# One attention-and-FFN kernel on one core: the plan's transfers re-costed, and the order of all engines drawn anew

## The chip, the core and the metric

The kernel runs on one core of a Trainium2 chip. The core has a matrix engine (PE, with its weight loads shown apart as PEld), a vector engine (DVE), a scalar engine (ACT), GpSimd (POOL), and a sync engine (SP) that here does nothing but issue transfers. The metric is the device time of one execution, in microseconds (us). Three executions of the kernel before took 928.43, 929.65 and 935.46 us.

## The reference, cut to what matters

```python
# q, k, v: 8 batches x 8 heads x 576 x 64;  omega: 128 x 64
def phi(x):
    h = x @ omega.T - sum(x * x) / 2
    return exp(h - max(h)) / sqrt(128)
kv  = phi(k).T @ v                      # per head, 128 x 64
z   = phi(k).sum(over the sequence)
out = (phi(q) @ kv) / (phi(q) @ z + 1e-6)
x   = out as 4608 tokens x 512
y   = gelu_erf(x @ w_in) @ w_out        # 512 -> 2048 -> 512
```

## The kernel before, in words

The attention is cut into 32 units of two heads (`u0` to `u31`, four a batch). The FFN is cut into 18 blocks of 256 tokens; block n can start when the batches that hold its tokens are through attention. Units `u0` to `u7` are worked in fp32 (`pair`, `shared`, `kv`, `q_trans`, `num_plain`); from `u8` on, and from block 1 on, each fp32 factor is split into a high and a low half and multiplied in three passes (`proj`, `kv_split`, `num`, `product`, `mm2`). Blocks use a seven-product scheme for the first FFN product (`sw1`, then `comb_a` on ACT and `comb_b`, `comb_c` on DVE, then `sw2`). The weights come in 16 pieces of 1 MB (`w_load`), each rebuilt on ACT, DVE and POOL (`w_hi`, `w_lo`, `w_shift`, `w_round`, `w_max`) before use, and split later (`w_low` and others).

Nothing is scheduled at run time. The kernel first lists all operations with `op(engine, cost, function, ...)`, and each takes a number from the table `RANK` (L36). `Planner.run` (L275) sorts the operations of each engine by that number, and each engine works in that order on the chip: an instruction whose inputs are late holds all that stands behind it on its engine. The costs serve three ends only: the sequence in which engines' operations are written down, which of several PSUM rings a result goes to, and the fillers. A filler is a matmul of no use, written by `put` (L1515) ahead of a PE operation for which the plan sees over 0.9 us of idle time:

```python
if X['fill'] and o.idle > 0.9 and o.t > 5.0:
    for _ in range(int((o.idle - 0.3) * X['fill'] / 0.11) if t else 0):
        nc.tensor.matmul(t[0][:, 0:256], id16[:, 0:P], id16, start=True, stop=True)
```

Transfers go out on SP's queue, in SP's order; only the transposed keys of `u0` and `u1`, and half of omega, go out on ACT's queue (`load_two` L746, `load_om` L517). SP and ACT each issue in their own order. DVE and POOL share a port to SBUF for some operations, which the planner knows by the names in `PORT` (L211) and by `port` in `run`.

Of the kernel before, what the change touches and what calls it, by code (L numbers as in the profile page):

```python
# [19 lines left out]
P = 128  # L20
# [10 lines left out]
X = dict(pm=0.15, tsw=1.28, psw=0.057, pst=0.3, plain=8, tiles=6, fill=0.6, kvp=8, eb0=8, amax=0, tc=1.2, tx=2.0)  # L31
# [4 lines left out]
RANK = (1, 0, 0, 0, 0, 1, 2, 2, 4, 6, 1, 4, 2, 3, 1, 3, 6, 6, 6, 8, 10, 12, 9, 7, 14, 21, 24, 3, 10, 15, 12, 16, 11, 14, 14, 20, 17, 23, 0, 3, 7, 2,  # L36
# [192 lines left out]
class Planner:  # L229
# [10 lines left out]
    def op(self, e, c, fn, *a, r=(), w=(), new=(), due=None, kind=None, tab=None, size=0, after=None, deps=()):  # L240
        o = Op()
# [136 lines left out]
def favor_attention_ffn(ctx: ExitStack, tc: tile.TileContext, qT, kT, v, omT, w_in, w_out, out):  # L378
# [12 lines left out]
    R2 = 2 * S  # L391
# [519 lines left out]
    def unit_plain(u):  # L911
        for s in range(2):
            op('SP', 0.05 if u.k < 2 and s == 0 else 0.45, load_two, u, s, w=[('x', s, u.k % 2)], size=295e3)
# [640 lines left out]
```

## Time and profile before

| | before |
|---|---|
| median of three runs | 929.65 us |
| lowest, highest | 928.43, 935.46 us |
| the profiled execution | 928.76 us |
| its span in the trace | 927.0 us |
| PE busy | 906.2 us, 98% of the span |
| ACT, DVE, POOL busy | 741.4, 736.2, 554.4 us |

A busy PE is one that has a matmul in its pipeline; matmuls overlap. The idle time that the views give before a group is that of its engine, with the work that ended it behind the arrow. The span is 1.8 us shorter than the execution's time.

### The profile page before, as it was taken

What the parts mean: (1) busy time and instruction counts of PE and PEld (TensorE: products, weight loads), DVE (VectorE), ACT (ScalarE), POOL (GpSimd) and SP (SyncE); (2) the same over time, 40 slices, a digit from 0 to 9 for tenths busy, and PEclk for the clock granted to TensorE, in tenths of its full rate; (3) what the DMA queues carried; (4) which work ended last, traced back from release to release, by engine and by line L of the source; (5) the groups of instructions that cost most, each with busy time, mean ns of one, the idle gap of its engine ahead of it and who ended that gap; (6) DMA issues with size and microseconds to landing.
All of it is one profiled execution on the core that took longest, in us unless ns stands there. A gap on an engine that the chain in (4) does not pass through costs nothing.

```text
span 927.0 us, 26668 instructions
## 1 busy us (share of the span) xinstructions
PE 906.2 (98%) x10045; PEld 705.7 (76%) x10045; DVE 736.2 (79%) x2378; ACT 741.4 (80%) x1590; POOL 554.4 (60%) x809
## 2 busy tenths in 40 slices
PE   7999999999999999999999999999999999999998
PEld 6897777587776777677777687768776777678997
DVE  4588999988987898788767898799879787757654
ACT  5898989799998988887879887999899756556553
POOL 1246578777787656755568546778687526533432
PEclk9799999999999999999999999999999999999999
DMA  8786522455555653645524655464643230222001
GB/s 259 190 254 212 174 52 78 122 115 134 121 133 112 133 114 92 141 107 93 138 66 90 157 78 157 99 138 116 139 101 74 50 85 19 63 36 53 24 3 46
DMA packets 165168, 101.27 MB, mean 109 GB/s; under 512 B 132528, under 2 KB 141104, under 8 KB 165040
## 3 DMA queue, kind: packets, MB, share of 16 engines
q1 hardware_dynamic: 164672, 98.95, 45.1%
q8 instruction: 79, 1.29, 0.6%
q10 hardware_dynamic: 368, 0.62, 0.3%
q14 instruction: 49, 0.40, 0.2%
HBM read 60.36 MB, written 9.44 MB: 75 GB/s over the span
## 4 chain that ended last, share of the span: by engine, by line
PE 81%; DVE 8%; ACT 7%; issue 2%; POOL 2%; DMA 1%; ACTq 0%; DVEq 0%; POOLq 0%
PE h L1200 30%; PE acc L1309 8%; PE acc L1310 8%; PE acc L1311 8%; PE at L965 4%; PE h L1187 3%; PE acc L1302 3%; PE acc L1264 3%; PE at L1264 2%; PE at L856 2%; PE at L1012 2%; DVE w L1002 1%; PE at L846 1%; PE at L761 1%; POOL r L957 1%
## 5 line engine op out<-in xcount | busy, mean ns | idle before, releaser
L957 POOL TENSOR_TENSOR r<-xt,r 64x256 fp32r<-64x256 f32 (+1 forms) x240 | 177.9, 753 | 102.4 <-ACT r L952 84.3
L1200 PE MATMUL h<-xh,w 128*128 128x128 f16 x3264 | 236.4, 219 | 0.0
L1200 PE MATMUL h<-xh,wih 128*128 128x128 f16 x1632 | 197.3, 220 | 3.6 <-DVE h L1217 3.0
L1200 PEld LDWEIGHTS <-w 128*128 128x128 f16 x3264 | 195.9, 98 | 3.5 <-issue 0.6
L1310 PE MATMUL acc<-woh,gl 128*128 128x512 f16 x448 | 170.0, 379 | 0.7 <-DVE gl L1299 0.7
L1309 PE MATMUL acc<-woh,gh 128*128 128x512 f16 x448 | 170.6, 381 | 0.0
L1311 PE MATMUL acc<-wol,gh 128*128 128x512 f16 x448 | 170.0, 379 | 0.0
L1200 PE MATMUL h<-xh,wil 128*128 128x128 f16 x816 | 155.6, 219 | 0.0
L1200 PEld LDWEIGHTS <-wih 128*128 128x128 f16 x1632 | 138.5, 98 | 12.7 <-DVE h L1217 3.0
L965 PE MATMUL at<-om,r 128*128 128x256 f32 x432 | 106.4, 345 | 5.2 <-DVE nm L974 2.2
L1299 DVE SCALAR_TENSOR_TENSOR gl<-h,bs,gh 128x512 f16<-128x512 f32 x116 | 86.3, 746 | 26.2 <-ACT gh L1234 25.6
L952 ACT CAST r<-xt 128x256 fp32r<-128x256 f32 (+1 forms) x240 | 89.6, 388 | 21.2 <-PE at L965 14.5
L969 ACT COPY lo<-at 128x256 f32<-128x256 f32 (+1 forms) x240 | 82.1, 353 | 18.9 <-DVE nm L974 8.3
L1225 ACT ACTIVATE h<-h,bs 128x512 f32<-128x512 f32 x116 | 76.6, 663 | 22.3 <-PE h L1200 16.5
L965 PEld LDWEIGHTS at<-om,r 128*128 128x128 f32 x432 | 71.2, 190 | 26.6 <-issue 4.5
L1311 PEld LDWEIGHTS <-gh 128*128 128x128 f16 x464 | 45.4, 98 | 54.3
L1200 PEld LDWEIGHTS <-wil 128*128 128x128 f16 x816 | 80.0, 98 | 8.5 <-issue 3.4
L1234 ACT ACTIVATE gh<-h,bs 128x512 f16<-128x512 f32 x116 | 80.1, 691 | 5.1 <-PE acc L1311 3.6
L1207 ACT COPY g<-h 128x256 f32<-128x256 f32 x136 | 50.7, 374 | 32.8 <-PE h L1200 30.2
L1309 PEld LDWEIGHTS <-gh 128*128 128x128 f16 x464 | 45.2, 97 | 35.4 <-ACT gh L1234 0.2
L1310 PEld LDWEIGHTS <-gl 128*128 128x128 f16 x464 | 45.5, 98 | 34.8 <-DVE gl L1299 2.1
L974 DVE CUSTOM_DVE_ANT_0 et<-at,lo 128x128 f32<-128x128 f32 x234 | 57.6, 283 | 14.5 <-ACT lo L969 14.0
(235 smaller groups left out, 2103.5 us busy)
## 6 DMA issues: line engine op xcount, KB each, us to landing
xt<-in_qT SPq DMA_DIRECT2D x56, 288.0 KB, 4.4
xt<-in_kT SPq DMA_DIRECT2D x54, 288.0 KB, 4.0
out_x<-o SPq DMA_DIRECT2D x35, 256.0 KB, 2.8
raw<-in_w_in SPq DMA_DIRECT2D x16, 512.0 KB, 5.7
raw<-in_w_out SPq DMA_DIRECT2D x16, 512.0 KB, 4.2
w<-in_v SPq DMA_DIRECT2D x24, 320.0 KB, 4.2
vt<-in_v SPq DMA_DIRECT2D x8, 320.0 KB, 6.6
qpad<-qc SPq DMA_TRANSPOSE x48, 3.3
```

What stands on the lines that cost most here:

```text
L952: nc.scalar.copy(G['r', u, i][:, 0:b - a], xf[:, a:b])
L957: nc.gpsimd.tensor_tensor(r, xf[D:, a:b], r, op=ALU.subtract)
L965: nc.tensor.matmul(o[:, t], r[:, t * P:(t + 1) * P], om, start=True, stop=True)
L969: nc.scalar.copy(G['lo', u, i][:, 0:n], pp_k(u, i)[:, 0:n, 1])
L974: nc.vector.tensor_tensor_reduce(u.et[:, t], pp_k(u, i)[:, t - t0, 0], G['lo', u, i][:, t - t0], 1.0, -3e38, ALU.add, ALU.max, G['nm', u][ ...
L1200: nc.tensor.matmul(h, w[p], x[r], start=first and i + m == 0, stop=last and i == 1 and m == 2, skip_group_check=True)
L1225: nc.scalar.activation(h, h, AF.Gelu, scale=G['bs', n][:, 2:3])
L1234: nc.scalar.activation(G['gh', n, c], G['h', n, c], AF.Copy, scale=G['bs', n][:, 3:4])
L1299: nc.vector.scalar_tensor_tensor(G['gl', n, c], G['h', n, c], G['bs', n][:, 3:4], G['gh', n, c], op0=ALU.mult, op1=ALU.subtract)
L1309: nc.tensor.matmul(acc, gh, woh[:, f, c0:c1], start=f == 0, stop=False, skip_group_check=True)
L1310: nc.tensor.matmul(acc, gl, woh[:, f, c0:c1], start=False, stop=False, skip_group_check=True)
L1311: nc.tensor.matmul(acc, gh, wol[:, f, c0:c1], start=False, stop=f == NF - 1, skip_group_check=True)
```

## The change: what it does

The operations stay the same, and so do their shapes, tiles and buffers. Two things are altered. The planner's costs of transfers get a size and an offset of their own for each kind, SP's clock in the plan may not run more than `ahead` = 4.5 us before the transfers in flight, and some ten costs of ACT and DVE operations are set anew. And the table `RANK` is replaced, so the order differs on all five engines.

```diff
-X = dict(pm=0.15, tsw=1.28, psw=0.057, pst=0.3, plain=8, tiles=6, fill=0.6, kvp=8, eb0=8, amax=0, tc=1.2, tx=2.0)
+X = dict(pm=0.15, tsw=1.28, psw=0.057, pst=0.3, plain=8, tiles=6, fill=0.6, kvp=8, eb0=8, amax=0, ahead=4.5)
-RANK = (1, 0, 0, 0, 0, 1, 2, 2, 4, 6, 1, 4, 2, 3, 1, 3, 6, 6, 6, 8, 10, 12, 9, 7, 14, 21, 24, 3, 10, 15, 12, 16, 11, 14, 14, 20, 17, 23, 0, 3, 7, 2,
+RANK = (1, 0, 0, 0, 0, 1, 25, 0, 4, 6, 1, 2, 3, 3, 2, 3, 6, 5, 6, 9, 9, 8, 10, 7, 12, 23, 23, 3, 10, 15, 12, 16, 11, 14, 14, 21, 17, 24, 3, 5, 7, 2,
...
+        o.off = off
...
-                free['SP'] = t + o.c
-                self.dma = max(self.dma, t + o.c + 1.9) + o.size / 340e3
+                free['SP'] = max(t + o.c, self.dma - X['ahead'])
+                self.dma = max(self.dma, free['SP'] - o.c + o.off) + o.size / 340e3
...
-        wl[0] = op('SP', 0.95, w_load, pc, new=[('raw', rk)], size=1048e3, after=wl[0])
+        wl[0] = op('SP', 0.95, w_load, pc, new=[('raw', rk)], size=1048e3, off=2.3, after=wl[0])
...
-            op('DVE', 0.98 if u.split else 1.2, norm, u, hh, r=[('pn', u, hh), ('dn', u)] + vr + old, w=[('dn', u, hh)] + [('xt', g, u.b, u.j, hh) for g in gs], new=new)
+            op('DVE', 1.05 if u.split else 1.02 if u.b == 0 else 1.45, norm, u, hh, r=[('pn', u, hh), ('dn', u)] + vr + old, w=[('dn', u, hh)] + [('xt', g, u.b, u.j, hh) for g in gs], new=new)
...
-            op('SP', 1.3, load_dup, u, s, w=[('x', s, a) for a in range(2)], size=590e3)
+            op('SP', 1.45, load_dup, u, s, w=[('x', s, a) for a in range(2)], size=720e3, off=3.2)
```

What the new table does to the order is shown at three places. The lines of the changed kernel stand one below those of the kernel before (L746 there is L747 here).

The first place is the start, on the two engines that issue transfers. `in_kT` and `in_qT` are the transposed keys and queries; in ACT's queue of the kernel before, the first `xt<-in_kT` is that of `u1` and the second that of `u0`. L558 loads a weight piece in two halves, L742 a unit's values. SP before:

```order
L517 DMA om_66<-in_omT 64x128
L746 DMA xt<-in_qT 128x576 x2
L558 DMA raw<-in_w_in 128x4x256 x2
L742 DMA vt_74<-in_v 128x10x64
L742 DMA vt_75<-in_v 128x10x64
L746 DMA xt<-in_kT 128x576 x2
```

SP in the change:

```order
L518 DMA om_66<-in_omT 64x128
L559 DMA raw<-in_w_in 128x4x256 x2
L747 DMA xt<-in_qT 128x576 x2
L743 DMA vt_74<-in_v 128x10x64
L743 DMA vt_75<-in_v 128x10x64
L559 DMA raw<-in_w_in 128x4x256 x2
L747 DMA xt<-in_kT 128x576
```

ACT in the change (`raw<-raw` is `w_hi`, `w_71<-raw` is `w_lo`, L778 the exponentials of a fp32 unit):

```order
L747 DMA xt<-in_kT 128x576
L518 DMA om_66<-in_omT 64x128
L521 ACT_TABLE_LOAD
L521 ACTIVATE pre_t<-ones 1x1
L747 DMA xt<-in_kT 128x576
L563 ACTIVATE raw<-raw 128x1024
L778 ACTIVATE et<-at,nm 128x128 x8
L566 ACTIVATE w_71<-raw 128x1024
```

The first weight piece now stands ahead of the queries on SP. On ACT the keys of `u0` are issued first and those of `u1` only behind the table load; `w_hi` of the first piece stands ahead of the first exponentials. Before, ACT issued both loads of keys ahead of the table load, and `w_hi` stood behind 14 exponentials.

The second place is DVE in block 1, ahead of `sw2(1,5)`, the sixth of eight such products. L1212 and L1213 are `comb_b(1,5)`, L1217 is `comb_c(1,5)`, L616 is `s_low`, L584 is `w_low`, and L864 to L873 are `norm`. Before:

```order
L873 TENSOR_TENSOR xk_84<-at_1805,dn_1745 128x4x64
L873 TENSOR_TENSOR xk_84<-at_1805,dn_1745 64x64
L616 SCALAR_TENSOR_TENSOR w32_71<-ts_1710,wsc_81,w32_71 128x512
L584 SCALAR_TENSOR_TENSOR wol_70<-w32_71,wsc_81,woh_69 128x512
L1212 TENSOR_TENSOR g_1893<-h_1765,g_1830 128x128
L1213 TENSOR_TENSOR h_1765<-h_1765,g_1893 128x256
L1217 TENSOR_TENSOR h_1765<-h_1765,g_1830 128x128
```

In the change:

```order
L1213 TENSOR_TENSOR g_1851<-h_1764,g_1837 128x128
L1214 TENSOR_TENSOR h_1764<-h_1764,g_1851 128x256
L865 TENSOR_SCALAR dn_1745<-at_1831 128x4
L866 RECIPROCAL dn_1745<-dn_1745 128x4
L865 TENSOR_SCALAR dn_1745<-at_1831 64x1
L866 RECIPROCAL dn_1745<-dn_1745 64x1
L874 TENSOR_TENSOR xk_84<-at_1831,dn_1745 128x4x64
L874 TENSOR_TENSOR xk_84<-at_1831,dn_1745 64x64
L585 SCALAR_TENSOR_TENSOR wol_70<-w32_71,wsc_81,woh_69 128x512
L1218 TENSOR_TENSOR h_1764<-h_1764,g_1837 128x128
```

`comb_b` has moved ahead of the `norm` and of `w_low`, and the `s_low` behind `comb_c`; `w_low` still stands ahead of `comb_c`.

The third place is PE ahead of `kv_split(u12)` (L1012). L1309 to L1311 are `mm2`, L1515 are fillers, L965 is `proj`. Before:

```order
L1310 MATMUL acc_3527<-woh_69,gl_4081 128x512
L1311 LDWEIGHTS gh_3988
L1311 MATMUL acc_3527<-wol_70,gh_3988 128x512
L1515 LDWEIGHTS ident_64
L1515 MATMUL at_4228<-ident_64 128x256
...
L1012 LDWEIGHTS w32_71
L1012 MATMUL at_4228<-w32_71 128x129
```

In the change:

```order
L1312 MATMUL acc_3527<-wol_70,gh_3974 128x512
L966 MATMUL at_4218<-om_65,r_4030 128x256 x2
L1310 LDWEIGHTS gh_3974
L1310 MATMUL acc_3553<-woh_69,gh_3974 128x512
...
L1312 MATMUL acc_3553<-wol_70,gh_3974 128x512
L1013 LDWEIGHTS w32_71
L1013 MATMUL at_4240<-w32_71 128x129
```

Two matmuls of `proj` and six of `mm2` now stand where seven fillers stood. In all the program before has 18 fillers: 11 ahead of `kv(u0)` and these 7. The changed program has 10, ahead of the second operation of PE after the warm-up, `pair(u1,0)`. All other counts of instructions are equal, engine by engine and line by line. At the very end, SP's last three stores before are of 128, 256 and 128 KB, and in the change of 128, 128 and 256 KB. Elsewhere most operations are a few places away from where they stood.

## Rows read from the trace of the kernel before

**Rows 1.** The page: busy time of each engine, share of the span, instructions.

```profile
PE 906.2 (98%) x10045; PEld 705.7 (76%) x10045; DVE 736.2 (79%) x2378; ACT 741.4 (80%) x1590; POOL 554.4 (60%) x809
```

**Rows 2.** Busy time by stretch: stretch, length, each engine's busy us, granted clock, DMA.

```profile
0.00:25.00 25.00, 19.12 (x181) 16.38 (x183) 9.85 (x26) 14.82 (x44) 3.06 (x7) 0.93 0.91 262
...
150.00:175.00 25.00, 23.72 (x223) 16.90 (x221) 24.17 (x73) 19.14 (x47) 20.20 (x29) 1.00 0.31 85
175.00:200.00 25.00, 23.40 (x277) 18.04 (x275) 23.04 (x74) 22.41 (x49) 19.84 (x29) 1.00 0.77 179
...
250.00:300.00 50.00, 46.74 (x537) 34.58 (x537) 42.59 (x173) 44.61 (x106) 40.95 (x64) 1.00 0.60 138
...
900.00:927.00 27.00, 23.10 (x251) 20.90 (x248) 12.83 (x29) 10.13 (x21) 4.95 (x10) 0.99 0.11 40
```

**Rows 3.** PE's waits over the span: us in total, times, longest.

```profile
PE h L1200 <- DVE h L1217: 3.0, 4, 1.3
```

**Rows 4.** PE in time order, first 17 us: start, us, what, idle before.

```profile
1.05 3.81 PE L513 MATMUL h<-w 128*128 128x256 bf16 x17 [1.05 <-DVE w L504]
8.32 2.12 PE L761 MATMUL at<-om,xt 64*128 64x128 f32 x17 [3.46 <-DMA xt<-in_kT]
...
14.94 1.37 PE L1515 MATMUL h<-ident 128*128 128x256 bf16 x11
16.15 2.18 PE L793 MATMUL h<-vt,et 128*128 128x65 f32 x18
```

**Rows 5.** Transfers issued from 0.7 to 1.2 us: size, us from issue to landing.

```profile
xt<-in_kT ACTq DMA_DIRECT2D x1, 288.0 KB, 3.2
```

**Rows 6.** The same for 1.7 to 2.35 us, then for 2.45 to 3.5 us.

```profile
xt<-in_kT ACTq DMA_DIRECT2D x1, 288.0 KB, 6.5
raw<-in_w_in SPq DMA_DIRECT2D x2, 512.0 KB, 8.0
```

**Rows 7.** ACT in time order, 0 to 26 us.

```profile
2.36 1.28 ACT L520 ACT_TABLE_LOAD   x1 [2.36 <-issue]
...
11.06 2.17 ACT L777 ACTIVATE et<-at,nm 128x128 f32<-128x128 f32 x8 [7.21 <-DVE nm L773]
...
15.47 1.14 ACT L562 ACTIVATE raw<-raw 128x1024 f32<-128x1024 f32 x1
```

**Rows 8.** Busy time by stretch, cut where the granted clock changed.

```profile
8.50:11.90 3.40, 3.40 (x32) 3.21 (x31) 1.29 (x2) 0.84 (x4) 0.00 (x0) 0.50 1.14 272
11.90:25.50 13.60, 12.23 (x138) 11.00 (x136) 7.23 (x13) 12.99 (x42) 2.35 (x1) 1.00 0.96 285
25.50:35.80 10.30, 10.30 (x60) 8.89 (x61) 4.62 (x19) 7.31 (x23) 2.55 (x2) 0.50 0.56 156
```

**Rows 9.** DVE, then POOL, in time order near 162 us.

```profile
160.82 1.02 DVE L616 SCALAR_TENSOR_TENSOR w<-ts,wsc,w 128x512 f16<-128x512 f32 x1
161.76 2.60 DVE L584 SCALAR_TENSOR_TENSOR wol<-w,wsc,woh 128x512 f16<-128x512 f32 x1
161.37 2.44 POOL L978 TENSOR_TENSOR et<-et,nm 128x1152 f32<-128x1152 f32 x1
```

**Rows 10.** Line 584 and line 1031: duration ns, least/median/most; first and last start.

```profile
L584 DVE SCALAR_TENSOR_TENSOR wol<-w,wsc,woh x16: 735/802/2596, 132.5 to 170.5; 128x512 f16<-128x512 f32 x16
L1031 DVE SCALAR_TENSOR_TENSOR kvl<-kvz,kvh x24: 281/290/2140, 212.7 to 754.7; 128x130 f16<-128x130 f32 x24
```

**Rows 11.** PE in time order near 282 us.

```profile
280.07 0.38 PE L1309 MATMUL acc<-woh,gh 128*128 128x512 f16 x1
...
281.36 0.93 PE L1515 MATMUL at<-ident 128*128 128x256 bf16 x7
283.65 1.03 PE L1012 MATMUL at<-w 128*128 128x129 f16 x18 [1.36 <-DVE w L994]
```

**Rows 12.** Stores: of the whole span, then the last one (issued after 924 us).

```profile
out_x<-o SPq DMA_DIRECT2D x35, 256.0 KB, 2.8
...
out_x<-o SPq DMA_DIRECT2D x1, 128.0 KB, 2.0
```

More of the change, by code (lines that the diff above doesn't have):

```diff
@@ L238, in ring, with op @@
         self.rings[name] = (bufs, [])
-    def op(self, e, c, fn, *a, r=(), w=(), new=(), due=None, kind=None, tab=None, size=0, after=None, deps=()):
+    def op(self, e, c, fn, *a, r=(), w=(), new=(), due=None, kind=None, tab=None, size=0, after=None, deps=(), off=2.0):
         o = Op()
+        o.off = off
         o.e, o.c, o.fn, o.a, o.new, o.own, o.kind, o.tab, o.size = e, c, fn, a, list(new), due, kind, tab, size
@@ L815, in bound @@
     def bound(u, key, more=()):
-        op('ACT', 0.16, bound_a, u, r=[key, *more], new=[('zr', ('zr', u))])
+        op('ACT', 0.2, bound_a, u, r=[key, *more], new=[('zr', ('zr', u))])
         op('DVE', 0.26, bound_b, u, r=[key], w=[('zr', u)], new=[('km', ('km', u))])
@@ L908, in out_ops @@
             started.update(gs)
-            op('DVE', 0.98 if u.split else 1.2, norm, u, hh, r=[('pn', u, hh), ('dn', u)] + vr + old, w=[('dn', u, hh)] + [('xt', g, u.b, u.j, hh) for g in gs], new=new)
+            op('DVE', 1.05 if u.split else 1.02 if u.b == 0 else 1.45, norm, u, hh, r=[('pn', u, hh), ('dn', u)] + vr + old, w=[('dn', u, hh)] + [('xt', g, u.b, u.j, hh) for g in gs], new=new)
     def unit_plain(u):
         for s in range(2):
-            op('SP', 0.05 if u.k < 2 and s == 0 else 0.45, load_two, u, s, w=[('x', s, u.k % 2)], size=295e3)
-        op('SP', 0.5, load_v, u, r=['vt1s'], w=[u.vk], size=327e3)
+            op('SP', 0.05 if u.k < 2 and s == 0 else 0.42, load_two, u, s, w=[('x', s, u.k % 2)], size=330e3)
+        op('SP', 0.55, load_v, u, r=['vt1s'], w=[u.vk], size=430e3, off=2.2)
         nm, ring = ('nm', u), ANY if u.b == 0 else ('at', 'h')
@@ L1073, in batch_v @@
         for u in us:
-            op('SP', 0.35, load_vst, u, r=['vstf'], w=[u.vk], size=327e3)
+            op('SP', 0.5, load_vst, u, r=['vstf'], w=[u.vk], size=340e3, off=2.5)
             op('DVE', 0.74, v_max, u, r=[u.vk], w=[('vm', b)])
@@ L1077, in batch_v @@
         op('POOL', 1.5, v_scales, b, r=[('exp', b, 0)], new=[('vsc', ('vsc', b))])
-        op('ACT', 0.3, v_spread, b, w=[('vsc', b)])
+        op('ACT', 0.42, v_spread, b, w=[('vsc', b)])
     def split_pre(u):
         for s in range(2):
-            op('SP', 1.3, load_dup, u, s, w=[('x', s, a) for a in range(2)], size=590e3)
+            op('SP', 1.45, load_dup, u, s, w=[('x', s, a) for a in range(2)], size=720e3, off=3.2)
         if u.kp:
-            op('SP', 0.5, load_v, u, r=['vt1s'], w=[u.vk], size=327e3)
+            op('SP', 0.55, load_v, u, r=['vt1s'], w=[u.vk], size=430e3, off=2.2)
         nm = ('nm', u)
@@ L1093, in split_pre @@
             op('ACT', 0.07 + n / 1200, proj_lo, u, i, r=[('pp', u, i)], new=[('lo', ('lo', u, i))])
-            op('DVE', 0.23 * n / P, proj_add, u, i, r=[('pp', u, i), ('lo', u, i)] + [nm], w=es + [nm + (i,)])
+            op('DVE', 0.02 + 0.215 * n / P, proj_add, u, i, r=[('pp', u, i), ('lo', u, i)] + [nm], w=es + [nm + (i,)])
         for a in range(2):
@@ L1117, in split_post @@
         qe, qc = [('et', u.eb, t) for t in range(NT, 2 * NT)], ('qc', u)
-        op('ACT', 0.16 + R2 / 1000, q_high, u, r=qe, new=[('qc', qc)])
+        op('ACT', 1.12, q_high, u, r=qe, new=[('qc', qc)])
         op('DVE', 0.1 + 0.13 * NT, q_low, u, r=qe + [qc], w=[qc + (1,)])
         for a in range(2):
-            op('SP', X['tc'], q_turn, u, a, r=[qc] + [qc + (1,)] * a, new=[(('qf', 'ql')[a], (('qf', 'ql')[a], u))], size=X['tx'] * 295e3)
+            op('SP', 1.35, q_turn, u, a, r=[qc] + [qc + (1,)] * a, new=[(('qf', 'ql')[a], (('qf', 'ql')[a], u))], size=600e3, off=1.7)
         out_ops(u)
@@ L1339, in block_prep @@
         op('POOL', 1.7, block_scales, n, r=[('be', n), ('exp', b0, 1), ('wsc', 1)], new=[('bs', ('bs', n))], kind='B')
-        op('ACT', 0.3, block_spread, n, w=[('bs', n)], kind='B')
+        op('ACT', 0.42, block_spread, n, w=[('bs', n)], kind='B')
         op('POOL', 0.31, block_out, n, r=[('bs', n), ('wsc', 0)], w=[('bo', n)])
@@ L1351, in block_prep @@
                 k = p // 2
-                op('SP', X['tc'], block_turn, n, k, r=[xc] + [xc + (q, l) for q in (p - 1, p) for l in range(2)] + [('xh', n)] * k, w=[('xh', n, k)],
-                   new=[] if k else [('xh', ('xh', n))], size=X['tx'] * (393e3, 524e3)[k])
+                op('SP', 1.55, block_turn, n, k, r=[xc] + [xc + (q, l) for q in (p - 1, p) for l in range(2)] + [('xh', n)] * k, w=[('xh', n, k)],
+                   new=[] if k else [('xh', ('xh', n))], size=(800e3, 1060e3)[k], off=1.7)
     def ffn_first(n, c):
@@ L1385, in ffn_first @@
             return
-        op('ACT', 0.15 + 512 / 1000, gelu, n, c, r=[('bs', n)], w=[hk], tab='g', kind='F')
-        op('ACT', 0.6, g_high, n, c, r=[('bs', n), hk], new=[('gh', ('gh', n, c))], kind='F')
+        op('ACT', 0.6, gelu, n, c, r=[('bs', n)], w=[hk], tab='g', kind='F')
+        op('ACT', 0.59, g_high, n, c, r=[('bs', n), hk], new=[('gh', ('gh', n, c))], kind='F')
         op('DVE', 0.66, g_low, n, c, r=[('bs', n), hk, ('gh', n, c)], new=[('gl', ('gl', n, c))], kind='F')
@@ L1415, in ffn_second @@
                             op('DVE', 0.12 + (min(c1, end) - c0) / 960, o_last, n, i, c0, min(c1, end), r=[('acc', n, 2 + i, 0)], w=[('o', n, i, c0)] + [('o', n, i)] * (n < NBLK - 1))
-                        op('SP', 0.35, store_dma, n, i, c0, c1, r=[('o', n, i), ('o', n, i, c0)], size=262e3 * (c1 - c0) / DM)
+                        op('SP', 0.45, store_dma, n, i, c0, c1, r=[('o', n, i), ('o', n, i, c0)], size=270e3 * (c1 - c0) / DM)
             return
@@ L1428, in ffn_second @@
                        new=[] if c0 else [('o', ('o', n, i))], due=(1, n + 1, (lag + i * .6) / nc_, 0.0), kind='F' if n >= N32 else 'F0')
-                    op('SP', 0.35, store_dma, n, i, c0, c1, r=[('o', n, i)], size=262e3 * (c1 - c0) / DM, due=(1, n + 1, (lag + 1) / nc_, 0.0))
+                    op('SP', 0.45, store_dma, n, i, c0, c1, r=[('o', n, i)], size=270e3 * (c1 - c0) / DM, due=(1, n + 1, (lag + 1) / nc_, 0.0))
     def p2():
```

346 rows, old and new, of the table RANK are left out of this document.

## The prediction

> **What bounds the kernel now.** I read the page first. PE is busy 98% of the span, 906.2 of 927.0 us [rows 1], and no other engine over 80%. The operations and their shapes stay, so PE's work stays; only its idle time of 20.8 us, its fillers and its slow clock can be won. Then I looked for the idle time stretch by stretch [rows 2]: 5.9 us lie in the first 25 us, and 3.9 us in the last 27, nearly all after the last matmul. The remaining 10.9 us lie in the middle: 1.3 us in 150 to 175, 1.6 in 175 to 200, 3.3 in 250 to 300, and 4.7 in stretches not shown. The order in time and the list of waits say what PE waited for. At the start it is a transfer, 3.46 us [rows 4]. In the middle it is DVE and POOL, for instance the `comb_c` of DVE in four waits of 3.0 us together [rows 3]; no transfer ended a wait of PE there. Last, the granted clock: it fell to 1.2 GHz for 3.4 us after the wait at the start, and for 10.3 us from 25.5 us on [rows 8].
>
> So the new account of transfers can act directly at one place, the start. Elsewhere the change acts by drawing the order anew.
>
> **The change, part by part**, against the profiled execution's 928.76 us; the median shown, 929.65 us, is 0.9 us above it.
>
> *The start.* PE ended the warm-up at 4.86 and began `pair(u0)` at 8.32 us [rows 4]. The first keys issued on ACT landed 3.2 us after their issue, near 4.0 us [rows 5]; the second, those of `u0`, 6.5 us after theirs [rows 6]. Now the first are those of `u0`, so `pair(u0)` can begin at about 4.9 us. The keys of `u1` are issued behind a table load of 1.28 us [rows 7], so at about 3.2 us. For their landing the nearest row is 6.5 us, which also had a megabyte queued beside it, so 9.7 us; as fast as the first it would be 6.4 us. The first weight piece, 1 MB, now stands ahead of the queries on SP. Behind two loads of queries it landed in 8.0 us [rows 6]; issued at about 1.4 us, it lands at 9.4 us by that row, and I take 9 us, since less stands ahead of it. The queries follow it on SP's queue at some 10 and 11 us, if 288 KB take 1 us at the 272 GB/s of that stretch [rows 8]; `pair(u1)` covers that from 9.7 us on.
>
> ACT runs `w_hi` of that piece, 1.14 us [rows 7], ahead of the first exponentials, so they begin at 10.2 us where they began at 11.06 [rows 7]. But `w_hi`, which stood in the middle of them, is then done. ACT is ahead by 0.9 + 1.1 = 2.0 us, and ACT is what counts here: in 11.9 to 25.5 us it was busy 12.99 of 13.6 us [rows 8], and `kv(u0)` at 16.15 us stood behind 11 fillers [rows 4], since it waited for exponentials. I take **2.0 us gained**. The most is the whole wait of 3.46 us. The least is nothing: if the piece lands 2 us later than I take, all of ACT's queue stands behind `w_hi`, and PE behind ACT.
>
> *The clock.* In 25.5 to 35.8 us PE was busy all the time at 1.2 GHz [rows 8]. At 2.4 GHz its matmuls would take half, but ACT had 7.3 us of work there, so that at most 3.0 us come back before ACT binds. The fall came after a stretch with only 1.4 us of scattered waits [rows 8]. The same fp32 work with short waits for ACT stands there after the change, so I take **nothing**; the bounds are 3.0 us gained, and 1.7 us lost if another 3.4 us run at half speed.
>
> *The wait before `kv_split(u12)`.* PE spent 2.3 us there, 0.93 in seven fillers and 1.36 idle, waiting for `v_b` [rows 11]. `v_b` comes no earlier, but now six `mm2` matmuls, which take 1.3 us (280.07 to 281.36 [rows 11]), and two of `proj` stand in the fillers' place: **1.5 us gained**, at most 2.3.
>
> *The wait before `sw2(1,5)`*, most of the 1.3 us in 150 to 175 us. A `w_low`, 0.80 us in the median [rows 10], took 2.60 us while a POOL `shift` ran 2.44 us, and `comb_b` and `comb_c` stood behind it and behind an `s_low` of 1.02 us [rows 9]. Now the `s_low` stands behind `comb_c` and `comb_b` is ahead: **1.0 us gained**, and nothing if `w_low` is stretched as much and one more operation comes late.
>
> *The other waits of the middle*, some 8 us. The order has moved at nearly all of them. They are of one kind: a DVE or POOL operation that is stretched, or queued ahead of the one PE wants. A new order loses old ones and meets new ones, and I see no row that says which are more. For the two that I took out I count two new ones of 0.75 us, the mean of the four in [rows 3]: **1.5 us lost**. The bounds are all 8 us gained and 15 us lost (20 new waits of that size).
>
> *The end.* SP's last store is of 256 KB, which takes 2.8 us, where 128 KB took 2.0 us [rows 12]: **0.8 us lost**.
>
> The remaining new costs act on fillers and PSUM rings alone. The ten fillers before `pair(u1)` take some 1.3 us (11 took 1.37 [rows 4]) in a wait from about 6.7 to 9.7 us, so they cost nothing; were the keys there at 6.4 us, they would cost their 1.3 us.
>
> The sum: -2.0 - 1.5 - 1.0 + 1.5 + 0.8 = -2.2, and 928.76 - 2.2 = **926.5 us**, 0.3% under the median. What a measurement of this kernel can tell from no change is about 1%, 9.3 us.
>
> **The rivals.**
>
> *The new order meets far fewer collisions.* For it: at the places that I followed, the awaited DVE operation mostly stands earlier. Against it: what made the waits is operations that took longer than planned, and a new order is drawn from a plan as well. All of the middle's 10.9 us gone, the fillers' 0.9, the start's whole 3.46 and half of the clock's 3.0, less 0.8: 928.8 - 16.0 = 912.8 us; with half of the middle gone 918.2 us. Chance 0.2.
>
> *DVE gives it back: slower.* From 150 us on DVE is busy 24.17 of 25 us, then 23.04 of 25 [rows 2]. If PE comes there 2 us earlier and DVE can't, an operation that POOL stretches (2.60 for 0.80 us, 2.14 for 0.29 [rows 10]) holds up PE as it did before `sw2(1,5)`, by 0.75 us in the mean and 1.3 at most [rows 3]. The gains less the end are 3.7 us, so five such waits use them up, and 20 give 928.8 - 3.7 + 15 = 940 us. Against it: DVE is busy for only 9.85 of the first 25 us [rows 2] and has room for work that is brought forward. Chance 0.2. The Trainium skill, page "SBUF — State Buffer", section "SBUF: two separate sides", says that DVE and GpSimd share a port pair, that the first to start holds it for its whole instruction, and that the other fully blocks; by that one hit may cost as much as a whole POOL operation, 2.44 us [rows 9], and two would use up the gain. The 2.60 us agree with it for DVE, while PE's longest such wait was 1.3 us.
>
> *The clock stays up.* If the long wait at the start was behind both falls, its end gives 3.0 us more: 923.5 us. Against it stands that PE was busy for nine tenths of the stretch before the second fall [rows 8]. Chance 0.1. The Trainium skill, page "TensorE: Matmul & The Clock Gate", section "Part 1: The HAM clock gate", has the clock fall once PE has been idle for a while; by that alone the second fall would not be there, and the trace shows it.
>
> *The start gives nothing*, since the weight piece lands late and holds up ACT: 928.5 us. Chance 0.15.
>
> **The numbers.** The forecast has 0.35. It, the late piece and the clock lie within 1% of 929.65 us, as do the lesser halves of the first two rivals. Under 920.4 us lies most of the first rival and a little of the forecast's lower bounds; over 938.9 us half of the slower one. Faster by over 1%: 0.21. Within: 0.68. Slower: 0.11. The range that leaves out 2 in 10 is 915 to 937 us.
>
> **What will show it.** The first matmul after the warm-up at about 4.9 us, the second pair at 9 to 10 us, the first exponentials at 10.2 us, `kv(u0)` near 14.2 us. Half clock for some 10 of the first 50 us. PE idle for under 2.5 us in 250 to 300 us. The forecast is wrong if the idle time of PE in the middle is under 6 or over 16 us, or if the first exponentials begin after 11 us.

## The result, and the profile after

The kernel after took 916.66 us in the median of four executions (915.84 to 918.68), against 929.83 for the kernel before: a ratio of 0.985, with a 95% interval of 0.981 to 0.989. It is 13.2 us faster, inside the forecast's range but 9.8 us below its value of 926.5. The profiled execution took 916.21 us, with a span of 914.4 us, 12.6 us shorter than before.

First the page of the kernel after, busy time of each engine, which answers to [rows 1]:

```profile
PE 899.0 (98%) x10037; PEld 699.4 (76%) x10037; DVE 728.3 (80%) x2378; ACT 739.2 (81%) x1590; POOL 556.7 (61%) x809
```

PE's busy time fell by 7.2 us, though its operations are the same but for eight matmuls: a PE at half clock counts as busy. The rest of the 12.6 us is idle time, 20.8 us before and 15.4 us now. Busy time by stretch of the kernel after, first where [rows 8] have the clock, then the stretches of [rows 2]:

```profile
8.50:11.90 3.40, 2.82 (x36) 2.04 (x38) 1.78 (x4) 2.17 (x6) 0.00 (x0) 1.00 1.16 259
11.90:25.50 13.60, 12.47 (x134) 11.24 (x133) 7.63 (x17) 13.60 (x45) 2.40 (x2) 1.00 1.01 296
25.50:35.80 10.30, 10.07 (x99) 8.72 (x100) 8.21 (x35) 10.30 (x34) 4.86 (x3) 1.00 0.77 241
...
150.00:175.00 25.00, 25.00 (x225) 16.80 (x223) 24.09 (x68) 20.51 (x39) 21.00 (x31) 1.00 0.39 112
175.00:200.00 25.00, 24.60 (x308) 20.07 (x306) 21.89 (x90) 23.33 (x61) 20.52 (x28) 1.00 0.67 135
250.00:300.00 50.00, 48.32 (x581) 36.66 (x578) 44.62 (x172) 45.55 (x107) 42.45 (x65) 1.00 0.55 119
900.00:914.00 14.00, 10.15 (x93) 8.86 (x91) 5.24 (x10) 1.68 (x4) 0.97 (x2) 0.98 0.10 37
```

In this execution the clock never fell before the last matmuls: in 25.5 to 35.8 us PE did 99 matmuls where it did 60. From 150 to 900 us PE is idle for 6.9 us, before for 10.9. PE in time order in the first 17 us (start, us, what, idle before), against [rows 4]:

```profile
4.89 1.47 PE L762 MATMUL at<-om,xt 64*128 64x128 f32 x16
6.29 1.27 PE L1516 MATMUL at<-ident 128*128 128x256 bf16 x10
8.57 0.37 PE L762 MATMUL at<-om,xt 64*128 64x128 f32 x1 [1.02 <-DMA xt<-in_kT]
...
15.01 1.66 PE L794 MATMUL h<-vt,et 128*128 128x65 f32 x13 [0.91 <-ACT w L778]
```

And ACT, against [rows 7]:

```profile
9.73 1.11 ACT L563 ACTIVATE raw<-raw 128x1024 f32<-128x1024 f32 x1 [6.49 <-DMA raw<-in_w_in]
10.74 2.15 ACT L778 ACTIVATE et<-at,nm 128x128 f32<-128x128 f32 x8
```

PE's longest waits over the span (us in total, times, longest):

```profile
PE at L966 <- POOL r L958: 2.6, 3, 1.5
PE at L966 <- DVE nm L975: 1.4, 1, 1.4
PE h L1201 <- DVE h L1218: 1.1, 2, 0.6
```

The waits for `comb_c` fell from four of 3.0 us [rows 3] to two of 1.1. The two traces are best compared operation by operation. This is when the same operation of PE ended, worked out from both, in us:

```
                     before    after   apart
kv(u0)                18.33    17.29    1.04
kv(u2)                38.34    31.38    6.96
num_plain(u4,0)       60.19    53.50    6.69
sw2(2,0)             193.53   184.97    8.55
mm2(3,4,1)           279.23   269.15   10.07
sw2(4,0)             300.41   288.53   11.88
kv_split(u18)        438.24   424.61   13.63
sw2(10,2)            587.40   575.23   12.17
mm2(12,7,1)          732.89   719.54   13.35
m2_c(17,4)           920.15   907.21   12.95
end of the span      927.0    914.4     12.6
```

So the 12.6 us are 1.0 at the start, 5.9 between `kv(u0)` and `kv(u2)`, where the clock fell before, and 6.0 behind that, less 0.35 at the end. The 6.0 are there by 440 us; from then on the distance only wavers. Which of these parts is the clock's and which the order's, this table can't say, since both differ; s1 below can.

### The profile page after: what moved, and what is told of

Same layout as the page of the kernel before. It is cut to its first block, busy times and chain, and to the rows that moved or that the text cites. A ratio compares the mean times of both kernels' runs of the same rounds, so it can differ in the third digit from the quotient of the medians.

```text
span 914.4 us, 26629 instructions
## 1 busy us (share of the span) xinstructions
PE 899.0 (98%) x10037; PEld 699.4 (76%) x10037; DVE 728.3 (80%) x2378; ACT 739.2 (81%) x1590; POOL 556.7 (61%) x809
## 4 chain that ended last, share of the span: by engine, by line
PE 89%; ACT 5%; DVE 2%; DMA 2%; issue 1%; POOL 1%; SPq 0%; DVEq 0%; ACTq 0%; POOLq 0%
PE h L1201 33%; PE acc L1310 9%; PE acc L1311 9%; PE acc L1312 9%; PE at L966 5%; PE h L1188 3%; PE acc L1303 3%; PE acc L1265 3%; PE at L857 2%; PE at L1265 2%; PE at L1013 2%; PE at L847 1%; DMA xh<-xc 1%; PE h L794 1%; DMA raw<-in_w_in 1%
## 5 line engine op out<-in xcount | busy, mean ns | idle before, releaser
L958 POOL TENSOR_TENSOR r<-xt,r 64x256 fp32r<-64x256 f32 (+1 forms) x240 | 180.6, 763 | 108.8 <-ACT r L953 81.7
L1311 PE MATMUL acc<-woh,gl 128*128 128x512 f16 x448 | 169.8, 379 | 0.4 <-DVE gl L1300 0.4
L966 PE MATMUL at<-om,r 128*128 128x256 f32 x432 | 103.7, 342 | 4.0 <-POOL r L958 2.6
L970 ACT COPY lo<-at 128x256 f32<-128x256 f32 (+1 forms) x240 | 82.3, 354 | 18.0 <-PE at L966 13.6
L1213 DVE TENSOR_TENSOR g<-h,g 128x128 f32<-128x128 f32 x136 | 38.8, 285 | 41.3 <-ACT g L1208 40.5
L1311 PEld LDWEIGHTS <-gl 128*128 128x128 f16 x464 | 45.5, 98 | 33.5 <-DVE gl L1300 0.7
```

What stands on the lines that cost most here:

```text
L958: nc.gpsimd.tensor_tensor(r, xf[D:, a:b], r, op=ALU.subtract)
L966: nc.tensor.matmul(o[:, t], r[:, t * P:(t + 1) * P], om, start=True, stop=True)
L970: nc.scalar.copy(G['lo', u, i][:, 0:n], pp_k(u, i)[:, 0:n, 1])
L1311: nc.tensor.matmul(acc, gl, woh[:, f, c0:c1], start=False, stop=False, skip_group_check=True)
```

## The experiments

Beside the experiments the kernel before ran 69 more times. One kernel's times spread, and they go with the mean granted clock of each execution, so two figures count: the median, and the times at a clock of 0.998 or more. The kernel before was under 0.995 in 57 of 69 executions (most near 929.5 us) and at 0.998 or more in nine, with a median of 924.5 us (922.7 to 926.0).

### Was the wait at the start behind the falls of the clock?

s1_before_filled:

```diff
-        for i in range(17):
+        for i in range(45):
             nc.tensor.matmul(G['warm'][:, 0:256], z16[:, 0:P], z16, start=True, stop=True)
```

> The kernel before, with 45 warm-up matmuls in place of 17, so that PE works through the 3.46 us in which it waited for the first keys; order, transfers and all other work stay. Theory A (that long wait was behind both falls of the clock): the granted clock stays full in 8 to 36 us. From the aligned traces, the second slow stretch, 25.5 to 35.8 us, cost 5.9 us (kv(u2) ended 38.34 us before and 31.38 us after the change, 6.96 us apart, of which 1.04 us were there at kv(u0) already), so about 924 us, ratio 0.994. Theory B (the second fall has a cause of its own, in what PE did from 12 to 25 us): the first slow stretch of 3.4 us goes, the second stays, and at most 1 us is gained, 929 us, ratio 0.999.

Median 923.92 us (12 executions; ratio 0.9971, 0.9946 to 0.9996). Seven had a clock of 0.999 or more and took 922.1 to 924.2 us; five had 0.994 and took 927.9 to 929.1. Its profile is one of the first kind; busy time by stretch:

```profile
11.90:25.50 13.60, 12.50 (x130) 11.35 (x128) 8.13 (x15) 13.60 (x43) 2.35 (x1) 1.00 1.03 300
25.50:35.80 10.30, 10.30 (x105) 9.05 (x103) 8.60 (x32) 10.30 (x32) 3.99 (x3) 1.00 0.71 222
```

With the same order PE does 105 matmuls in 25.5 to 35.8 us, and ACT is busy throughout, where it had 7.31 us [rows 8]. Its operations on PE stand 1.0 us ahead of their times in the kernel before at `kv(u0)`, 5.9 us ahead at `kv(u2)`, still 5.8 at 340 and 6.0 at the end. So the two slow stretches of the kernel before cost 1.0 and 4.9 us. Theory A has the time right, but its 5.9 us for the second stretch alone are some 1 us too much: with the order unchanged that stretch costs 4.9, and the other 1.1 between `kv(u0)` and `kv(u2)` in the table above comes from the order. And `kv(u0)`, in the old order with its old transfers, begins within 0.13 us of the kernel after (at 15.27 and 14.84 us in s5 and s12 below, which have the 45 matmuls too):

```profile
15.14 2.17 PE L793 MATMUL h<-vt,et 128*128 128x65 f32 x18
```

As to the cause, neither theory holds alone: without the long wait falls are rarer (5 of 12 against 57 of 69; with s5 and s12, 13 of 36), but not gone.

s6_before_second and s5_before_both (the latter with the 45 warm-up matmuls too); 143 is `w_hi(w1.1)`, 53 the second of the two exponentials:

```diff
-            o.due = RANK[o.id]
+            o.due = {143: RANK[53] + 0.5}.get(o.id, RANK[o.id])
```

> The kernel before with only the w_hi(w1.1) moved; the wait of 3.46 us at the start stays. Theory A: the fall at 8 us stays, that at 25 us goes; clock 0.996 to 0.998, 924 us. Theory B (the long wait at the start is behind the later fall): the clock stays at 0.991 to 0.994 in most executions, 928.5 us.

> The kernel before with both causes of idle time ahead of the slow stretches removed: 45 warm-up matmuls, and on ACT w_hi(w1.1), 1.0 us, moved behind the two exponentials for which pair(u3) waited 1.36 us in two pieces. Theory A (each short wait of PE of about 1 us in the first 50 us can make the clock fall, in some executions): with none of over 0.5 us left the clock is 0.998 or more in at least 11 of 12 executions and the time is 922 us (s1 at full clock, 923.0, less the 1.0 us of the wait). Theory B (the falls come by chance, whatever PE waits): 0.994 in about 5 of 12 as in s1, at 927 us.

s6: median 927.69 us (ratio 0.9994, 0.9968 to 1.002), eight of 12 under 0.995, none at 0.998. s5: 923.53 us (0.9954, 0.9928 to 0.998), three of 12 under 0.995, eight at 0.999 or more with 922.0 to 924.2 us. Both miss their aim, as PE in time order shows in s5:

```profile
22.26 1.16 PE L761 MATMUL h<-om,xt 64*128 64x128 f32 x14 [0.16 <-ACT w L777]
24.40 1.36 PE L846 MATMUL h<-kvz,qh 128*128 128x65 f32 x10 [0.98 <-ACT qh L826]
```

The wait before `pair(u3)` went, and one of 0.98 us for the copies behind it on ACT came. So these two don't settle what the second wait does; s6 shows that with the long wait at the start the falls stay.

s4_after_late_key (7 and 38 are the two loads of keys):

```diff
-            o.due = RANK[o.id]
+            o.due = RANK[{7: 38, 38: 7}.get(o.id, o.id)]
```

> The kernel after, with the issues of the first two key loads on ACT exchanged: the keys of u1 come first, PE waits some 3.5 us for those of u0, and all else stays in the order after. Theory A (the long wait makes the clock fall, also later): half clock for 3 us from 8 us on and again for some 10 us within the first 40 us, 916.7 + 5 to 7 = 922 to 924 us. Theory B (the second fall came from the scattered waits before pair(u3)): half clock once, and 917 to 919 us, by the 0 to 2 us that the first exponentials begin later (before the change they began at 11.06 us, after it ACT's first work began at 9.73 us).

Median 919.22 us (six executions; 0.9903, 0.9873 to 0.9934); 917.3 to 918.6 at 0.998 or more. The edit made no idle time: the plan saw the wait and put 16 fillers into it.

```profile
4.65 3.10 PE L1516 MATMUL at<-ident 128*128 128x256 bf16 x16
8.04 1.24 PE L762 MATMUL at<-om,xt 64*128 64x128 f32 x17 [0.29 <-DMA xt<-in_kT]
```

So it says nothing on the long wait. In its trace the exchange of the two loads is worth little: `pair(u0)` began 3.15 us later than in the kernel after, and `kv(u0)` 0.2 us earlier. But its three executions at 0.998 or more are 2.2 us over the kernel after in the median, and this trace doesn't show why. In it the clock fell at 17.3 us, and at 181.2 us after a wait of 1.92 us for `gl`, a result of DVE.

### How much is the start, how much the rest?

s2_before_after_start (s3_after_before_start the other way round, 92 operations; `RANK_AFTER` is the other table, and `EARLY` lists the operations of the start):

```diff
-            o.due = RANK[o.id]
+            o.due = (0, RANK_AFTER[o.id]) if any(a <= o.id < b for a, b in EARLY) else (1, RANK[o.id])
```

> The first 89 operations of the plan (up to shared(u3), 29 us in the trace after the change) in the order after the change, all that follow in the order before. Theory A (the start and the clock are one gain, independent of what follows): 1.0 us at kv(u0) and 5.9 us by the full clock in 25 to 36 us, 929.8 - 6.9 = 923 us, ratio 0.9925. Theory B (the time won early is given back at the middle's waits, which the old order keeps and meets earlier): 926 to 930 us, ratio over 0.996. Under either the clock is full in the first 40 us.

> The mirror: the first 92 operations in the order before the change, all that follow in the order after. Theory A: the wait of 3.5 us before the first keys and both slow stretches are back, which costs 6.9 us: 916.7 + 6.9 = 923.6 us, ratio to before 0.993. Theory B (the early part is worth nothing, the middle gives all): 917 us, ratio 0.986.

s2: median 927.13 us (0.9983, 0.9949 to 1.0016). At 0.998 or more, six of 12, it took 922.8 to 924.9 us, 0.6 us under the kernel before in the median; at 0.987 to 0.992, 929 to 934. Theory A holds as far as 53 us, where PE is 6.3 us ahead of the kernel before; then the clock fell, as PE in time order and the stretches show:

```profile
50.59 0.33 PE L999 MATMUL h<-ident,et 128*128 128x128 f32 x1 [1.20 <-ACT w L1003]
```

```profile
46.00:53.00 7.00, 5.80 (x55) 5.11 (x54) 3.76 (x15) 7.00 (x22) 3.81 (x2) 1.00 1.01 289
53.00:66.60 13.60, 13.60 (x62) 12.31 (x62) 7.96 (x30) 8.06 (x13) 3.12 (x3) 0.50 0.59 175
```

At 60 us it is 1.3 us behind and so at the end: one fall, with the wait ahead of it, took 7.6 us. Theory A expected a full clock and Theory B named another mechanism; both fail in half of the executions.

s3: median 926.43 us (0.999, 0.9964 to 1.0016), ten of 12 at 0.994 or less; 921.1 and 921.6 us in the other two. The profile shows 1.6 us lost against the kernel after at 20 us, 8.3 us at 30 us, with waits of 1.58 and 0.55 us and a fall at 27.4 us, and 9.5 at the end. The old start costs more than Theory A's 6.9 us there; Theory B is out.

s7_after_again changes nothing.

> The kernel after, unchanged, for the share of its executions in which the clock falls. Theory A: its longest waits in the first 50 us are 1.02 and 0.91 us, shorter than the 1.36 us before, so falls are rarer than the 22 of 29 of the kernel before: 0.995 or less in 1 to 4 of 12, median 916.5 us. Theory B (falls by chance alike in every kernel): 8 or 9 of 12, median about 920 us.

Median 916.65 us (four executions, 915.30 to 917.23; 0.9866, 0.9833 to 0.99). With the first four, the clock of the eight is 0.995 to 1.0, none under 0.995: falls are rarer, and Theory B is out. One such fall is in its profile:

```profile
16.20:23.00 6.80, 6.80 (x40) 6.34 (x39) 1.94 (x5) 4.81 (x16) 1.20 (x1) 0.50 1.01 314
```

It puts PE from 1.1 us ahead of the first profile to 1.1 us behind at 51 us. The 1.1 us ahead go with the landing, in one and the same program: the weight piece was there at 8.58 us, not at 9.73, and `kv(u0)` began at 13.88 us, not at 15.01:

```profile
13.88 2.28 PE L794 MATMUL h<-vt,et 128*128 128x65 f32 x18 [0.91 <-ACT w L778]
```

At 0.998 or more the kernel after has a median of 916.2 us, 8.3 under the kernel before at such a clock and 6.8 under s1 at 0.999 or more. So some 7 to 8 us of the 13 are the order, and some 5 to 6 are the clock. What the start's order is worth is small beside them: 0.6 us by the medians of s2, 0.1 and 1.3 us at `kv(u0)` by the two profiles of the kernel after against s1.

s10_table_alone takes the kernel before with the new `RANK` and nothing else.

> The new table of order with all of the old durations and the old account of transfers. The order of every engine is that of the kernel after; what the plan thinks of idle time differs, and so it sets 38 fillers in place of 10, 8 of them at the start and 30 at seven places further on. Theory A (the order alone makes the gain; the fillers at the seven places stand in time in which PE works): 30 times 0.11 to 0.13 us, 3.3 to 3.9 us lost, 920.3 us. Theory B (they stand in waits and cost nothing): 916.7 us. Theory C (the new account of transfers matters beyond the order): 925 us or more.

Median 918.61 us (six executions; 0.9903, 0.9875 to 0.993), 918.1 at 0.998 or more. The order alone makes nearly all of the gain; Theory C is out. At 0.998 or more it is 1.9 us over the kernel after, not the 3.3 to 3.9 us that the 30 fillers would take: against the kernel after, PE is 2.9 us behind at 60 us, where a fall at 17.8 us is in it, and loses 2.2 us more by the end, some 0.3 to 0.7 us at a time. So part of them may have stood in waits; steps of this size also come without fillers (s11 below).

### Does a filled wait stay filled?

s12_one_wait (with 45 warm-up matmuls; 919 is `mm2(3,5,1)`, of six matmuls, 1591 `kv_split(u12)`):

```diff
-            o.due = RANK[o.id]
+            o.due = {919: RANK[1591] - 0.5}.get(o.id, RANK[o.id])
```

> One term of the forecast by itself, on the kernel before with 45 warm-up matmuls (it had 923.05 us at a full clock): three mm2 matmuls of the next piece, 1.3 us, are moved ahead of kv_split(u12), into the wait of 2.3 us in which seven fillers stood. Theory A (a wait that is filled in the middle stays won to the end): 1.3 us less at a full clock, 921.7 us. Theory B (the engine behind it, DVE, catches PE again within the next pieces): 923.0 us, with the operations of PE from about 320 us on at the same distance from their times in the kernel before as those ahead of 280 us.

Median 924.85 us (0.9981, 0.9954 to 1.0007); at 0.999 or more 924.1 us, against 923.05 for s1. Theory B holds, sooner than it says. PE in time order:

```profile
278.02 1.05 PE L1012 MATMUL at<-w 128*128 128x129 f16 x18 [0.83 <-DVE w L994]
279.91 0.39 PE L1309 MATMUL acc<-woh,gh 128*128 128x512 f16 x1 [0.37 <-ACT gh L1234]
281.05 0.39 PE L1310 MATMUL acc<-woh,gl 128*128 128x512 f16 x1 [0.75 <-DVE gl L1299]
```

The 2.3 us [rows 11] have become 0.83, 0.37 and 0.75: the work taken forward is missing behind `kv_split(u12)`, where PE now waits for the next pieces of ACT and DVE. Against s1 PE stands at -0.17 us before and after this place.

### Is there a better start?

s8_after_whi_later (137 is the first `w_hi`, 12 an exponential), s9_start_again (136 is the weight load, 39 the queries of `u1`, 45 an exponential of `u1`) and s11_no_fill:

```diff
-            o.due = RANK[o.id]
+            o.due = {137: RANK[12] + 0.5}.get(o.id, RANK[o.id])                                                    # s8
+            o.due = {136: RANK[39] + 0.50, 137: RANK[45] + 0.50, 138: RANK[45] + 0.60}.get(o.id, RANK[o.id])       # s9
```

```diff
-X = dict(..., fill=0.6, ...)
+X = dict(..., fill=0, ...)                                                                                          # s11
```

> The kernel after with one operation moved: on ACT the first w_hi, which waited for its weight piece until 9.73 us, stands behind the first two exponentials, whose maxima were ready on DVE near 7.1 and 7.7 us. Theory A (ACT sets the pace of the first 20 us): the first exponentials begin near 7.9 us in place of 10.74, kv(u0) begins at 14.1 in place of 15.01 us, when PE's pairs are done, and 0.9 to 1.3 us are gained: 915.5 us. Theory B (the weights' chain over DVE and POOL, now 1 us later, holds up the weight pieces that follow): 916.5 to 918 us.

> The kernel after with its start changed further: on SP the first weight piece of 1 MB stands behind the queries of u0 and u1 instead of ahead of them, and on ACT w_hi and w_lo of that piece stand behind the first five exponentials of u0 and u1. Theory A (the megabyte ahead of the keys and queries is what PE waits for until 8.57 us, and ACT until 9.73 us): the keys of u1 land near 6.5 us, shared(u0) runs near 8 us, kv(u0) begins near 12 us in place of 15.01, and 1.5 to 3 us are gained over the kernel after: 913.7 to 915.2 us. Theory B (ACT, busy all of 10 to 50 us, sets the pace and only its own start counts): as the kernel with w_hi moved alone, 914.7 us. Theory C (the weight chain comes too late for the first FFN block at 53 to 60 us): 917 us or more.

> The kernel after without its ten fillers; the order is the same, and PE stands idle for 2.3 us before pair(u1). Theory A (a wait of over 1 us in the first 50 us makes the clock fall): the granted clock falls in most executions, as in the kernel before (0.994 or less in 40 of 52), at a cost of 1 to 5 us by its place: 918 to 921 us. Theory B (the fillers do nothing): 916.7 us and the clock at 0.998 or more in half of the executions, as with them (5 of 8).

s8: median 914.74 us (four executions, 914.51 to 916.30; ratio to before 0.9852, 0.9818 to 0.9885), 1.9 us under s7 beside it; all four at a clock of 1.0. Against the five executions of the kernel after at 0.998 or more (915.3 to 917.1) it is 1.5 us. That is the time of Theory A, but the two groups overlap, and no trace shows where it comes from: the profile is of the execution of 916.3 us, in which omega was ready 1.1 us late on DVE, and PE is 0.3 us ahead of the kernel after at 20 us and 0.1 behind at the end. s9: 916.70 us (0.988, 0.9852 to 0.9909), no gain. The keys of `u1` still came at 8.73 us, so the megabyte ahead was not what held them up, and Theory A falls; the time lies between those of Theory B and Theory C. ACT began at 8.04 us but then waited for DVE, and `kv(u0)` began at 14.44:

```profile
8.73 0.38 PE L762 MATMUL at<-om,xt 64*128 64x128 f32 x1 [2.05 <-DMA xt<-in_kT]
```

```profile
12.32 0.62 ACT L778 ACTIVATE et<-acc,nm 128x128 f32<-128x128 f32 x2 [2.11 <-DVE nm L774]
```

s11: 914.75 us (five executions, 914.44 to 915.57; 0.9859, 0.9831 to 0.9887), all at a clock of 0.998 or more; 1.9 us under the eight executions of the kernel after, 1.5 under the five at such a clock. Neither theory expected it. Against the first profile of the kernel after PE is 0.5 us ahead at 15 us, where the weight piece came 0.5 us earlier, gains 0.6 near 600 us and 0.5 near 800, and ends 1.7 us ahead. The 0.6 near 600 is a wait of `proj` for POOL, 1.48 us long in the kernel after and 0.86 here. It is shorter in s9 too (0.73 us), with its fillers in, and s4 gains the 0.5 near 800 as well. This is the wait over the span in s11, then in s9; the kernel after has 2.6:

```profile
PE at L966 <- POOL r L958: 2.0, 3, 0.9
PE at L966 <- POOL r L958: 1.8, 3, 0.7
```

So these are steps that come with fillers and without, and that the fillers hold anything up isn't shown. s8 and s11 have the lowest medians of this study, some 14 us under the kernel before; both together weren't tried.

## Why the prediction was right or wrong, point by point

- **What bounds it.** Right. PE is at 98% in both, and no transfer ended a wait of PE in the middle.
- **The start: 2.0 us forecast, 1.0 measured** at `kv(u0)`, and not for the reason given. The steps came nearly as told: first matmul at 4.89 us, second pair at 8.57, first exponentials at 10.74 (10.2 forecast), since the weight piece came at 9.73 and not at 9. `kv(u0)` began at 15.01, not 14.2. But s1 has the 1.0 us with the old order: there the first slow stretch was gone, the first exponentials began at 10.62 us (11.06 before), and `kv(u0)` at 15.14. So what made the kernel before late was the half clock behind its long wait, which the forecast saw and gave no price of its own. The new order gave 0.1 us at `kv(u0)` in this profile, 1.3 in that of s7, where the piece came earlier, and 1.1 by `kv(u2)`. That the landing of the piece decides was forecast rightly.
- **The clock: nothing forecast, 5.9 us measured** by s1, 1.0 in the first slow stretch and 4.9 in the second. This step failed, in its value and in its bound. The value rested on one fall in one execution; in s1, with the same order, the clock stayed up in seven of 12. In the second stretch PE worked 10.3 us at half clock; at full clock the same work would take 5.15 us less by its length, near the 4.9. The bound of 3.0 took ACT's 7.31 us in that stretch as a floor, as if PE needed all of it. ACT also prepares weight pieces there, which nobody awaits before the first FFN block; s1's ACT was busy all the stretch and did not hold up PE. The rival "the clock stays up" named what happened, at some six tenths of its size; its condition, that the long wait was behind both falls, is borne out in part only (s1). The Trainium skill, page "TensorE: Matmul & The Clock Gate", section "Part 1: The HAM clock gate", says of the matmuls at low clock at a kernel's start that their number differs from run to run; the later falls here do so too (under 0.995 in 57 of 69 executions of the kernel before).
- **The wait before `kv_split(u12)`: 1.5 us.** In the change it is 0.50 us:

```profile
273.50 1.05 PE L1013 MATMUL at<-w 128*128 128x129 f16 x18 [0.50 <-DVE w L995]
```

  Between `mm2(3,4,1)` and `sw2(4,0)` the two kernels move 1.8 us further apart. But s12 shows that the cause I gave, other matmuls in the fillers' place, gives nothing by itself. In the change the engines behind it are earlier too; that this is what keeps the gain was not run by itself.
- **The wait before `sw2(1,5)`: 1.0 us forecast.** It is gone: PE is busy 25.00 of 25 us in 150 to 175, 1.3 us more than before.
- **The other waits of the middle: 1.5 us lost forecast.** Wrong in sign. From 150 to 900 us PE's idle time and fillers went from 11.9 to 6.9 us, 5.0 us in all, where I counted 1.0 for the middle with the two named waits. That is near the first rival with half of the middle gone. What goes with it is seen on DVE: over the span, 31 of its instructions took over 0.5 us more than the median of their kind before, and 19 after, while POOL has 24 and 28. In s2, with the old order behind the start, DVE has 33, and in s10, with the new table, 14. `w_low`, with a longest of 2596 ns [rows 10], now has 1316, as its duration over the span (least, median, most) shows:

```profile
L585 DVE SCALAR_TENSOR_TENSOR wol<-w,wsc,woh x16: 741/872/1316, 126.2 to 162.2; 128x512 f16<-128x512 f32 x16
```

  That these stretched instructions are the cause is argued, not shown, and which of the many moves did it was not tested one by one; s10 shows only that it is the order, and s2 that it is the order behind the start.
- **The rival "DVE gives it back".** It did not happen to what is won early: s1's lead of 5.8 us is there to the end. It did happen to the single filled wait of s12.
- **The end: 0.8 us lost forecast, 0.35 measured.** The last store, of 256 KB, took 2.0 us, not 2.8. The 2.8 is the median of 35 stores over the span; the one of 256 KB among the last three of the kernel before took 2.1.

So the sum missed the profiled execution by 10.3 us: 5.9 for the clock, 5.0 for the middle (1.0 forecast, 6.0 by the ends of the operations) and 0.4 for the end, with 0.9 the other way for the order of the start (2.0 forecast, 1.1 by `kv(u2)`). That the time still fell into the range is owed to the width that the first rival gave it (912.8 to 918.2 us), not to the sum.

## What to carry to other kernels

A fall of PE's clock is a term of the sum like any other: price it at up to the full difference of PE's work, ask which work of the other engines PE really awaits there, and look at several executions before saying that it stays. Where a planned order is drawn anew, compare when the same operations end: what is won at the start stays won, flat to the end, while work moved forward into one wait can leave a hole of the same size behind it. And before a gain at the start is put down to an order, run the old order with the clock held up: here one edit of the warm-up gave the same 1.0 us.

## What the runs showed of the hardware

The granted clock of one and the same program differed between executions: 0.984 to 1.0 for the kernel before, with 923 to 937 us. In the profiles a fall came soon after short waits of PE: waits of 0.82 and 0.55 us ahead of 25.5 us in the kernel before, 1.20 us ahead of 53.0 in s2, 1.92 us ahead of 181.2 in s4. But a wait of 1.5 us in the kernel after and one of 1.59 us near 500 us in s12 brought none, so what decides it stays open. Its price differs by length and place: 7.6 us for 13.6 us of half clock at 53 us (s2, with its wait), 4.9 for 10.3 at 25 us and 1.0 for 3.4 at 8.5 us (the kernel before, by s1), some 2 for 6.8 at 16 us (s7), and nothing that the time shows for 3.4 us at 7.7 us in s11. Landing times differ between executions as well: the first weight piece of the kernel after was there at 9.73 us in one profile and at 8.58 in the other.
